# First batch of a threshold attention: transposes by the identity instead of by scaled identities, and another rhythm of the weight conversion

## The chip, the cores and the metric

The kernel runs on one core of a Trainium2 chip. The metric is device microseconds of one execution, the median over several runs. The profile is one such execution, taken by the hardware profiler. In profiles PE is TensorE (its weight loads are PEld), DVE is VectorE, ACT is ScalarE, POOL is GpSimd and SP is SyncE.

## The reference

Two blocks follow each other, all in fp32 results (the three weight matrices arrive as 64-bit floats).

```
# attention: batch 8, heads 8, sequence 576, head size 64
scores = (q @ k^T) / sqrt(64)
thresh = max(scores, last axis) - tau
scores = where(scores >= thresh, scores, -1e9)
attn   = softmax(scores)              # sum + 1e-9 in the denominator
a      = attn @ v                     # (8, 8, 576, 64)
x      = heads side by side           # (4608, 512)
# SwiGLU: 512 -> 1536 -> 512
g   = x @ w_gate
out = (g * sigmoid(g) * (x @ w_val)) @ w_out
```

## The kernel before

**Work units.** The attention goes by head pairs: a pair is two heads of one batch entry, so there are 4 pairs a batch entry and 32 in all. The kernel strings them together as segments. The first batch entry is cut differently from the rest. Segments 0 to 3 hold tiles 0 and 1 (128 rows of q each) of pairs 0 to 3; segments 4 to 7 hold tiles 2, 3 and the short tile 4 (64 rows, both heads in one set of 128 partitions) of the same pairs. From segment 8 on a segment is a whole pair with five tiles, in the "halved" layout. Below, a tile is named by segment and place: 4x1 is the second tile of segment 4.

**One tile of the first batch** (`scores`, not halved). TensorE makes the scores (L301, L306) into two score banks of PSUM, one for each head. VectorE takes the row maximum, negated (`nm`, L326). ScalarE makes the threshold (`th`, L331) and the exponential (L332). VectorE masks it and sums the rows (L336), then makes the reciprocal of the sum (`ri`, L346). The score bank is free for the next tile when L336 has run. So far p is not normalised: ScalarE multiplies the identity matrix by `ri`, one per head (`diags`, L361), and the scaling is done by the transposes.

**The transposes** (`flip`). p has the rows of q on partitions and must have the columns on partitions for the product with v. `flip` does it on TensorE by ordinary products, p as the stationary operand and the scaled identity as the moving one: four blocks of 128x128 into one bank (L389), the last 64 columns into the `end` bank (L391, L395). ScalarE copies them to SBUF (L392, L396, L397). `attend_tile` multiplies them by v one tile later (L412, L416), and ScalarE copies the result into x (L418). From the second batch on none of this is used: there p is scaled by ScalarE (L354) and GpSimd (L352), and VectorE transposes it in 32x32 blocks (L371).

**The weights.** Each weight matrix comes as 64-bit words and must be turned into fp32. It is cut into 24 pieces: 16 of w_gate and w_val (each with 384 columns of both, for 128 rows), 8 of w_out. `fetch_weights` starts the transfers, `split_weights` makes two fp32 parts on ScalarE (L191, L192), `join_weights` puts them together with three operations on VectorE (L200, L202, L203) and one on GpSimd (L205). At most one piece is split in most tiles, and one joined: "one step per tile".

**The fill.** The SwiGLU products are cut into pieces by the generator `block`: `gate` (L481, `pg`), `value` (L481, `pv`), then the output products (L562 for the first two units, L595 for the others). `fill(part)` is called twice per tile and puts as many pieces into TensorE's queue as `pace` allows: the work that is at hand over the tiles that are left. A piece of gate with row block f needs the first 4, 8, 12 or 16 weight pieces; `need` makes them on the spot when they are not there. The first unit of rows is given to the fill in segment 4.

**Order.** All engines work their queues in program order, and the order is written by hand in the loop at the end of the kernel. For each tile: its scores up to the exponential; `attend_tile` for the tile two before; `flip` for the tile before; a weight split; masking and reciprocal; a weight join; fill; scaled identities; fill; and, at the last but one tile of a segment, `prepare` of the next segment (transposes of k and q on VectorE, L767 to L773) and the transfer of the q and k after that, with q multiplied by a constant on GpSimd (L244).

Of the kernel before, what the change touches and what calls it, by code (L numbers as in the profile page):

```python
# [13 lines left out]
AF = mybir.ActivationFunctionType  # L14
ALU = mybir.AluOpType
# [4 lines left out]
def kernel(  # L20
# [30 lines left out]
    nc = tc.nc  # L51
    P = 128
    B, H, S, D = q.shape
    NP = H // 2
# [154 lines left out]
    def need(n):  # L209
        while len(joined) < n:  # L210
            fetch_weights(2)
            if not split:
                split_weights()
            join_weights()
            split_weights()
# [61 lines left out]
    def scores(seg, t):  # L277
        qT, kT, tiles, halved = seg["qT"], seg["kT"], seg["tiles"], seg["halved"]
        if halved and "p" not in seg:
            seg["p"] = arenas[seg["i"] % 2]  # L280
        q0 = t * P - seg["q0"]
        heads = [slice(h * D, (h + 1) * D) for h in range(2)]
        if t < NT:
            pss = [ps_s.tile([P, 2, 512], F32, name="sc") for _ in range(2)]
            at = [t, NT + 1 + t]
        else:
            pss = [ps_s.tile([P, 2, 512], F32, name="sc")]
            at = [t]
        if halved:
            put = [(pss[u], h, q0 + u * D) for u in range(len(pss)) for h in range(2)]  # L290
            for x in range(0, len(put), 2):
                for g in range(NG):
                    a, c = divmod(g, 2)
                    for ps, h, col in put[x:x + 2]:
                        hs = heads[h]
                        nc.tensor.matmul(ps[g * G:(g + 1) * G, h, 0:SH], qT[hs, col + a * G:col + (a + 1) * G],  # L296
                                         kT[hs, c * SH:(c + 1) * SH], start=True, stop=True)
        elif t < NT:
            for h, hs in enumerate(heads):
                for n in range(2):  # L300
                    nc.tensor.matmul(pss[h][:, n, 0:SH], qT[hs, q0:q0 + P], kT[hs, n * SH:(n + 1) * SH],  # L301
                                     start=True, stop=True)
        else:
            for n, h in ((0, 0), (1, 1), (1, 0), (0, 1)):
                hs = heads[h]
                nc.tensor.matmul(pss[0][hs, n, 0:SH], qT[hs, q0:q0 + D], kT[hs, n * SH:(n + 1) * SH],  # L306
                                 start=True, stop=True)
        mx, nm, th, ri = (stp.tile([P, 4, 2] if x == "mx" else [P, 4], F32, name=x) for x in ("mx", "nm", "th", "ri"))
        sm = sums[0]
        sums.rotate(1)  # L310
        if halved:
            m = 2 * len(at)
            scs = [ps[:, h, 0:SH] for ps in pss for h in range(2)]
            ps = [seg["p"][:, x, u * SH:(u + 1) * SH] for u in range(2) for x in at]
            for x, tile_ in enumerate(pss):
                nc.vector.tensor_reduce(out=mx[:, 2 * x:2 * x + 2, 0], in_=tile_[:, :, 0:SH], axis=AX.X, op=ALU.max,  # L316
                                        negate=True)
            meet(mx, m, largest)
            nc.vector.tensor_reduce(out=nm[:, 0:m], in_=mx[:, 0:m, :], axis=AX.X, op=ALU.min)  # L319
        else:  # L320
            m = len(at)
            scs = [ps[:, :, 0:SH] for ps in pss]
            ps = [pbufs[0][:, x, :].rearrange("p (n s) -> p n s", n=2) for x in range(m)]
            pbufs.rotate(1)
            for x in range(m):
                nc.vector.tensor_reduce(out=nm[:, x:x + 1], in_=scs[x], axis=AX.XY, op=ALU.max, negate=True)  # L326
        if halved:
            nc.scalar.activation(th[:, 0:m], nm[:, 0:m], AF.Identity, bias=cut, scale=-1.0)  # L328
        for x in range(m):
            if not halved:  # L330
                nc.scalar.activation(th[:, x:x + 1], nm[:, x:x + 1], AF.Identity, bias=cut, scale=-1.0)  # L331
            nc.scalar.activation(ps[x], scs[x], AF.Exp, bias=nm[:, x:x + 1])  # L332
        yield
        turn(1)
        for x in range(m):
            nc.vector.scalar_tensor_tensor(out=ps[x], in0=scs[x], scalar=th[:, x:x + 1], in1=ps[x],  # L336
                                           op0=ALU.is_ge, op1=ALU.mult, accum_out=sm[:, x, 0:1])
        tot = stp.tile([P, 4], F32, name="tot")
        if halved:
            yield  # L340
            meet(sm, m, same)
            yield
            nc.vector.tensor_reduce(out=tot[:, 0:m], in_=sm[:, 0:m, :], axis=AX.X, op=ALU.add)
        else:
            nc.vector.tensor_reduce(out=tot[:, 0:m], in_=sm[:, 0:m, 0:3:2], axis=AX.X, op=ALU.add)
        nc.vector.reciprocal(out=ri[:, 0:m], in_=tot[:, 0:m])  # L346
        if not halved:
            yield
        if halved:
            for x in range(m):  # L350
                if x % 2:
                    nc.gpsimd.tensor_scalar(out=ps[x], in0=ps[x], scalar1=ri[:, x:x + 1], scalar2=None, op0=ALU.mult)  # L352
                else:
                    nc.scalar.activation(ps[x], ps[x], AF.Copy, scale=ri[:, x:x + 1])  # L354
            unturned.append([seg["p"][:, x, :] for x in at])
        else:

            diags = dbufs[0][:, 0:m, :]
            dbufs.rotate(1)
            for x in range(m):  # L360
                nc.scalar.activation(diags[:, x, :], ident, AF.Copy, scale=ri[:, x:x + 1])  # L361
            unflipped.append((seg, t, [(p.rearrange("p n s -> p (n s)"), diags[:, x, :]) for x, p in enumerate(ps)]))
            yield
        yield

# [10 lines left out]
    def flip():  # L376

        if not unflipped:
            return
        seg, t, ps = unflipped.popleft()  # L380
        n = P if t < NT else D
        pT = pTbufs[0][:, 0:2 * KT * n].rearrange("p (h t q) -> p h t q", h=2, t=KT)
        pT2 = pTbufs[0][:, 2 * KT * n:(2 * KT + 1) * n]
        pTbufs.rotate(1)
        end = ps_f.tile([P, 512], F32, name="end", tag="psf")
        for h, (p, diag) in enumerate(ps):
            tp = ps_f.tile([P, 512], F32, name="tp", tag="psf")
            for kt in range(KT):
                nc.tensor.matmul(tp[:, kt * P:(kt + 1) * P], p[:, kt * P:(kt + 1) * P], diag, start=True, stop=True)  # L389
            if t < NT:  # L390
                nc.tensor.matmul(end[h * D:(h + 1) * D, 0:P], p[:, KM:S], diag, start=True, stop=True)  # L391
                nc.scalar.copy(pT[:, h], tp.rearrange("p (t q) -> p t q", q=P))  # L392
            else:
                for hs in (slice(0, D), slice(D, P)):
                    nc.tensor.matmul(end[hs, 0:D], p[hs, KM:S], diag[hs, hs], start=True, stop=True)  # L395
                nc.scalar.copy(pT, tp.rearrange("p (t h q) -> p h t q", h=2, q=D))  # L396
        nc.scalar.copy(pT2, end[:, 0:n])  # L397
        unattended.append((seg, t, pT, pT2))
# [88 lines left out]
    def gate(j, cs, f, hts, gts):  # L487
# [4 lines left out]
        if f % per == 0:  # L492
            gt = gp.tile([P, 2, TC], F32, name="gt").rearrange("p f n -> p (f n)")
            gts[f // per] = gt[:, 0:per * n].rearrange("p (f n) -> p f n", n=n)
        need(NCC * ((f + GR - 1) * P // FW + 1))
        ps = yield from rows_of_products(j, cs, f, 0, "pg")
        nc.scalar.copy(gts[f // per][:, f % per:f % per + GR, :], ps)  # L497
        yield HCOST
# [194 lines left out]
    def start_batch(b):  # L693
# [8 lines left out]
        if b % BT == 0:  # L702
            while ("last", b // BT - 1) in xts:
# [8 lines left out]

    flat = pall.rearrange("p n s -> p (n s)")
    pbufs = deque(pall[:, 8 + 2 * x:10 + 2 * x] for x in range(2))
    dbufs = deque(flat[:, NP * (S - QA) + 2 * P * x:NP * (S - QA) + 2 * P * (x + 1)].rearrange("p (h q) -> p h q", h=2)
                  for x in range(2))
    pTbufs = deque(flat[:, (12 + 2 * x) * S:(14 + 2 * x) * S] for x in range(2))
    segs = [{"i": i, "tiles": early, "halved": False} for i in range(NP)]
    segs += [{"i": i, "tiles": rest, "halved": False} for i in [NP - 1, *range(NP - 1)]]
    segs += [{"i": i, "tiles": ([2, 3, 0, 1] if i % 2 else [0, 1, 2, 3]) + [NT], "halved": True} for i in range(NP, NPAIR)]  # L720
    assert (2 * KT + 1) * P <= 2 * S and NP == NT == 4 and NP * (S - QA + P) <= 4 * S
    gains = []
    for n, seg in enumerate(segs):
        seg["gives"] = supply(n // NP - 1) if n % NP == NP - 1 and n >= NP else []
# [69 lines left out]
    for n, seg in enumerate(segs):  # L794
        if NP <= n < 2 * NP:
            seg["v"] = segs[seg["i"]]["v"]
        for x, t in enumerate(seg["tiles"]):
# [11 lines left out]
            if attends and n > 2 * NP:  # L809
# [2 lines left out]
                    start_batch(prev["i"] // NP)  # L812
                products = attend(prev)
            part = pace(n, x) / 2
            more = len(split)
            if n or x:
                split_weights()
                fetch_weights(2)
            if x == 0 and n >= NP:
                fetch_qk(seg["i"] + 1)  # L820
            next(go)
# [5 lines left out]
                sigmoids()  # L827
            fill(part)
            next(go)
            if attends and n > 2 * NP:  # L830
                next(products)
                next(products)
                give(n - 1)
# [49 lines left out]
```

## Time and profile before

| | |
|---|---|
| time | 1569.68 us, median of 3 runs (1569.26 to 1570.92) |
| span in the profile | 1568.6 us, granted TensorE clock 0.991 |
| instructions | 31607 |
| first scores of tile 0x1 | 13.03 us from the start |
| first scores of tile 4x1 | 69.45 us |
| first scores of the second batch (segment 8) | 157.97 us |

The page gives, for the whole span, the busy time of each engine and its busy share in 40 slices of 39 us each. The tables of windows give busy us by engine for any stretch. In a timeline, a line has start, duration, engine, line of the kernel, operation, what it writes and reads, and in brackets how long its engine was idle before it and what released it.

### The profile page before, as it was taken

The numbers are of one execution on the slowest core, as the hardware profiler recorded it, in microseconds if no ns is written. First come the engines' busy times: TensorE is split into PE (matmuls) and PEld (weight loads), VectorE is DVE, ScalarE is ACT, GpSimd is POOL, SyncE is SP. The second block draws the span as 40 slices with busy tenths as digits, with TensorE's granted clock in tenths as the row PEclk, the third lists the DMA queues.
The fourth block names the chain that finished last, engine by engine and source line by source line (L and its number), as shares of the span: only waits on it lengthen the run. The fifth ranks groups of instructions, "written<-read, shape, count | busy, mean of one in ns | idle before, by whom it ended". The sixth has DMA issues, their size and how long they took to land. (4 is left out here: it accounts for less than half of the span.)

```text
span 1568.6 us, 31607 instructions
## 1 busy us (share of the span) xinstructions
PE 1509.2 (96%) x11872; PEld 1141.3 (73%) x11872; DVE 1022.2 (65%) x3150; ACT 832.2 (53%) x2165; POOL 628.3 (40%) x638
## 2 busy tenths in 40 slices
PE   7999878999999999999999999999999999899998
PEld 5777554467677767777777777777777777788887
DVE  6866877777677757774767777777676777412212
ACT  5767766546465555654555555474647464511110
POOL 2313543336546354633454544363536263500011
PEclk9999999999999999999999999999999999999999
DMA  8533311211111111110211111111011120000000
GB/s 189 142 99 102 95 28 31 56 43 30 24 45 45 31 32 45 43 34 1 45 32 45 31 45 31 45 32 36 12 42 31 45 46 15 1 14 0 14 14 14
DMA packets 176489, 66.93 MB, mean 43 GB/s; under 512 B 159696, under 2 KB 159696, under 8 KB 176336
## 3 DMA queue, kind: packets, MB, share of 16 engines
q1 hardware_dynamic: 168656, 54.88, 15.7%
q0 software_dynamic: 2944, 9.44, 1.7%
q8 instruction: 94, 1.54, 0.4%
q10 hardware_dynamic: 4736, 0.59, 0.3%
q14 instruction: 59, 0.48, 0.1%
HBM read 55.44 MB, written 9.44 MB: 41 GB/s over the span
## 5 line engine op out<-in xcount | busy, mean ns | idle before, releaser
L481 PE MATMUL pv<-xall,wgv 128*128 128x256 f32 x1728 | 405.7, 386 | 0.0
L481 PE MATMUL pg<-xall,wgv 128*128 128x256 f32 x1728 | 399.9, 382 | 0.0
L481 PEld LDWEIGHTS pv<-xall,wgv 128*128 128x128 f32 x1728 | 328.4, 192 | 67.0 <-issue 21.7
L481 PEld LDWEIGHTS pg<-xall,wgv 128*128 128x128 f32 x1728 | 323.5, 190 | 66.4 <-issue 19.0
L352 POOL TENSOR_SCALAR pall<-pall,ri 128x288 f32<-128x288 f32 x252 | 249.9, 1002 | 258.3 <-DVE ri L346 234.0
L336 DVE SCALAR_TENSOR_TENSOR pall<-sc,th,pall 128x288 f32<-128x288 f32 (+1 forms) x540 | 258.6, 529 | 63.6 <-ACT pall L332 63.6
L332 ACT ACTIVATE pall<-sc,nm 128x288 f32<-128x288 f32 (+1 forms) x540 | 236.1, 509 | 0.5
L296 PE MATMUL sc<-kT,qT 64*32 64x288 f32 x4032 | 161.6, 416 | 34.8 <-DVE pall L336 33.3
L316 DVE TENSOR_REDUCE mx<-sc 128x2 f32<-128x576 f32 x252 | 177.7, 742 | 22.3 <-PE sc L296 21.1
L371 DVE STREAM_TRANSPOSE pall<-pall 128x576 f32<-128x576 f32 x252 | 181.9, 754 | 10.7 <-POOL pall L352 10.7
L522 POOL TENSOR_TENSOR ht<-ht,gt 128x512 f32<-128x512 f32 x84 | 104.7, 1272 | 200.9 <-ACT gt L520 200.9
L275 ACT COPY sums<-sums 32x4 f32<-32x4 f32 (+1 forms) x560 | 108.5, 194 | 143.7 <-DVE pall L336 134.2
L595 PE MATMUL po<-wo,ht 128*128 128x256 f32 x768 | 176.8, 382 | 0.0
L595 PEld LDWEIGHTS po<-wo,ht 128*128 128x128 f32 x768 | 144.9, 191 | 28.0 <-issue 4.6
L354 ACT ACTIVATE pall<-pall,ri 128x288 f32<-128x288 f32 x252 | 122.2, 527 | 69.6 <-DVE ri L346 68.5
L504 DVE TENSOR_TENSOR ht<-gt,pv 128x512 f32<-128x512 f32 x102 | 69.8, 685 | 125.0 <-PE pv L481 116.2
L328 ACT ACTIVATE th<-nm,cut 128x4 f32<-128x4 f32 (+1 forms) x140 | 41.2, 295 | 206.1 <-DVE nm L319 206.0
L296 PEld LDWEIGHTS sc<-kT,qT 64*32 64x32 f32 x4032 | 58.6, 106 | 114.7 <-issue 83.5
L438 PE MATMUL xa<-pall,vall 64*64 64x288 f32 x2016 | 130.2, 405 | 0.7 <-issue 0.6
L438 PEld LDWEIGHTS xa<-pall,vall 64*64 64x64 f32 x2016 | 77.8, 133 | 49.1 <-issue 5.8
L608 POOL TENSOR_TENSOR ht<-ht,xall 128x256 f32<-128x256 f32 x48 | 34.7, 726 | 184.5 <-PE po L595 182.2
L497 ACT COPY gt<-pg 128x512 f32<-128x512 f32 x108 | 63.5, 588 | 79.7 <-PE pg L481 77.3
(102 smaller groups left out, 1477.0 us busy)
## 6 DMA issues: line engine op xcount, KB each, us to landing
vall<-in_v_dram SPq DMA_DIRECT2D x112, 144.0 KB, 3.4
qraw<-in_q_dram SPq DMA_DIRECT2D x116, 72.0 KB, 2.5
kraw<-in_k_dram SPq DMA_DIRECT2D x116, 72.0 KB, 2.9
out_dram<-ob POOLq DMA_DIRECT2D x32, 256.0 KB, 2.4
wo<-in_moe_w_gate_dram SPq DMA_DIRECT2D x16, 384.0 KB, 3.8
wo<-in_moe_w_val_dram SPq DMA_DIRECT2D x16, 384.0 KB, 4.3
xall<-in_moe_w_out_dram SPq DMA_DIRECT2D x5, 768.0 KB, 4.6
wo<-in_moe_w_out_dram SPq DMA_DIRECT2D x3, 768.0 KB, 4.8
```

The source lines that it names most:

```text
L275: nc.scalar.copy(out, in_[:, :, 0])
L296: nc.tensor.matmul(ps[g * G:(g + 1) * G, h, 0:SH], qT[hs, col + a * G:col + (a + 1) * G], kT[hs, c * SH:(c + 1) * SH], start=True, stop=True)
L316: nc.vector.tensor_reduce(out=mx[:, 2 * x:2 * x + 2, 0], in_=tile_[:, :, 0:SH], axis=AX.X, op=ALU.max, negate=True)
L332: nc.scalar.activation(ps[x], scs[x], AF.Exp, bias=nm[:, x:x + 1])
L336: nc.vector.scalar_tensor_tensor(out=ps[x], in0=scs[x], scalar=th[:, x:x + 1], in1=ps[x], op0=ALU.is_ge, op1=ALU.mult, accum_out=sm[:, x, ...
L352: nc.gpsimd.tensor_scalar(out=ps[x], in0=ps[x], scalar1=ri[:, x:x + 1], scalar2=None, op0=ALU.mult)
L354: nc.scalar.activation(ps[x], ps[x], AF.Copy, scale=ri[:, x:x + 1])
L371: nc.vector.transpose(out=p, in_=p)
L438: nc.tensor.matmul(xa[a][h * D:(h + 1) * D, at:at + n * G].rearrange("d (i q) -> d i q", q=G), vr[rs, h, j, :], p[rs, lo:lo + n, j, :], st ...
L481: nc.tensor.matmul(ps[:, i], wgv[:, mat, c, (f + i) * P:(f + i + 1) * P], x[:, c, cs], start=(c == 0), stop=(c == NCC - 1))
L522: eng.tensor_tensor(out=ht, in0=ht, in1=gt[:, 2 * y:2 * y + 2, :], op=ALU.mult)
L595: nc.tensor.matmul(ps, h(f), w[:, f, :], start=(f == 0), stop=(f == NF2 - 1))
```

## The change

Three edits, all for the first batch. The transposes use the identity in TensorE's transpose mode, so p is scaled beforehand: the first head of a tile by ScalarE, the second by GpSimd, as in the later batches; the scaled identities and their buffers go. The weight steps get another rhythm: in segments 0 to 3 one per two tiles, with the split and the join in the same (second) tile; from segment 4 on one per tile, and in segments 4 to 7 a second one in the short tile. And a gate piece whose weights are not joined yet makes the fill pass instead of forcing them.

```diff
         nc.vector.reciprocal(out=ri[:, 0:m], in_=tot[:, 0:m])
-        if not halved:
-            yield
+        for x in range(m):
+            if x % 2:
+                nc.gpsimd.tensor_scalar(out=ps[x], in0=ps[x], scalar1=ri[:, x:x + 1], scalar2=None, op0=ALU.mult)
+            else:
+                nc.scalar.activation(ps[x], ps[x], AF.Copy, scale=ri[:, x:x + 1])
         if halved:
...
         else:
-
-            diags = dbufs[0][:, 0:m, :]
-            dbufs.rotate(1)
-            for x in range(m):
-                nc.scalar.activation(diags[:, x, :], ident, AF.Copy, scale=ri[:, x:x + 1])
-            unflipped.append((seg, t, [(p.rearrange("p n s -> p (n s)"), diags[:, x, :]) for x, p in enumerate(ps)]))
+            unflipped.append((seg, t, [p.rearrange("p n s -> p (n s)") for p in ps]))
+            yield
             yield
         yield
...
-        for h, (p, diag) in enumerate(ps):
+        for h, p in enumerate(ps):
             tp = ps_f.tile([P, 512], F32, name="tp", tag="psf")
             for kt in range(KT):
-                nc.tensor.matmul(tp[:, kt * P:(kt + 1) * P], p[:, kt * P:(kt + 1) * P], diag, start=True, stop=True)
+                nc.tensor.transpose(tp[:, kt * P:(kt + 1) * P], p[:, kt * P:(kt + 1) * P], ident)
             if t < NT:
-                nc.tensor.matmul(end[h * D:(h + 1) * D, 0:P], p[:, KM:S], diag, start=True, stop=True)
+                nc.tensor.matmul(end[h * D:(h + 1) * D, 0:P], p[:, KM:S], ident, start=True, stop=True)
...
-        need(NCC * ((f + GR - 1) * P // FW + 1))
+        while len(joined) < NCC * ((f + GR - 1) * P // FW + 1):
+            yield 0
...
             more = len(split)
-            if n or x:
+            if n >= NP or x:
                 split_weights()
                 fetch_weights(2)
+            if n < NP:
+                more = x
...
             fill(part)
             next(go)
+            if t == NT and NP <= n < 2 * NP:
+                join_weights()
+                split_weights()
+                fetch_weights(2)
```

More of the change, by code (lines that the diff above doesn't have):

```diff
@@ L346, in scores @@
         nc.vector.reciprocal(out=ri[:, 0:m], in_=tot[:, 0:m])
-        if not halved:
-            yield
-        if halved:
-            for x in range(m):
[L351 to L354, printed above, removed]
+        for x in range(m):
[3 more added lines that the diff above has]
+                nc.scalar.activation(ps[x], ps[x], AF.Copy, scale=ri[:, x:x + 1])
+        if halved:
             unturned.append([seg["p"][:, x, :] for x in at])
         else:
-            diags = dbufs[0][:, 0:m, :]
-            dbufs.rotate(1)
-            for x in range(m):
-                nc.scalar.activation(diags[:, x, :], ident, AF.Copy, scale=ri[:, x:x + 1])
-            unflipped.append((seg, t, [(p.rearrange("p n s -> p (n s)"), diags[:, x, :]) for x, p in enumerate(ps)]))
+            unflipped.append((seg, t, [p.rearrange("p n s -> p (n s)") for p in ps]))
+            yield
             yield
@@ L394, in flip @@
                 for hs in (slice(0, D), slice(D, P)):
-                    nc.tensor.matmul(end[hs, 0:D], p[hs, KM:S], diag[hs, hs], start=True, stop=True)
+                    nc.tensor.matmul(end[hs, 0:D], p[hs, KM:S], ident[hs, hs], start=True, stop=True)
                 nc.scalar.copy(pT, tp.rearrange("p (t h q) -> p h t q", h=2, q=D))
@@ L714 @@
     pbufs = deque(pall[:, 8 + 2 * x:10 + 2 * x] for x in range(2))
-    dbufs = deque(flat[:, NP * (S - QA) + 2 * P * x:NP * (S - QA) + 2 * P * (x + 1)].rearrange("p (h q) -> p h q", h=2)
-                  for x in range(2))
     pTbufs = deque(flat[:, (12 + 2 * x) * S:(14 + 2 * x) * S] for x in range(2))
@@ L720 @@
     segs += [{"i": i, "tiles": ([2, 3, 0, 1] if i % 2 else [0, 1, 2, 3]) + [NT], "halved": True} for i in range(NP, NPAIR)]
-    assert (2 * KT + 1) * P <= 2 * S and NP == NT == 4 and NP * (S - QA + P) <= 4 * S
+    assert (2 * KT + 1) * P <= 2 * S and NP == NT == 4
     gains = []
```

## The prediction

> **What bounds the kernel now.** I read the page first (engine shares, slices), then a table of three stretches, then TensorE's waits in each, then the timeline of one tile. From the page:
>
> ```profile
> PE 1509.2 (96%) x11872; PEld 1141.3 (73%) x11872; DVE 1022.2 (65%) x3150; ACT 832.2 (53%) x2165; POOL 628.3 (40%) x638
> PE   7999878999999999999999999999999999899998
> ```
>
> TensorE is busy nearly throughout, so work taken from it counts wherever it never waits. The first slices (39 us each) and the dip at slices 5 and 6 are the places where it may wait. The change touches only the first batch: segments 0 to 3 (two tiles each), segments 4 to 7 (three tiles each), and a little of what follows. I cut there: first scores of tile 0x1 (segment 0, tile 1) to those of 4x1, from there to the first scores of the second batch, and onward. Busy us of each engine:
>
> ```profile
> core 0: us, PE busy (x) PEld busy (x) DVE busy (x) ACT busy (x) POOL busy (x), PEclk, DMA share, GB/s
> 13.03:69.45 56.42, 55.25 (x400) 41.44 (x400) 46.42 (x99) 43.71 (x98) 18.64 (x11) 1.00 0.73 186
> 69.45:157.97 88.52, 87.53 (x638) 66.41 (x637) 57.63 (x116) 61.06 (x128) 23.68 (x14) 1.00 0.31 98
> 157.97:330.00 172.03, 146.83 (x1277) 86.64 (x1280) 135.00 (x435) 109.07 (x291) 72.72 (x64) 0.95 0.23 53
> ```
>
> TensorE's waits, first in the middle stretch, then in the late one:
>
> ```profile
> PE tp L389 <- ACT xall L418: 0.8, 2, 0.4
> PE tp L389 <- ACT gt L497: 0.2, 1, 0.2
> ```
>
> ```profile
> PE sc L296 <- DVE pall L336: 23.5, 12, 3.4
> ```
>
> So there are three regimes. The middle stretch (88.5 us) is bound by TensorE: it waits 1.0 us in all, while VectorE and ScalarE have 31 and 27 us to spare. The late stretch has TensorE waiting 23.5 us for VectorE to free the score banks. The early stretch looks TensorE-bound by busy time, but the timeline of tiles 2x1 and 3x0 says otherwise:
>
> ```profile
> 47.78 1.72 POOL L244 TENSOR_SCALAR qraw<-qraw,scl 128x576 f32<-128x576 f32 x1 [4.10 <-DMA qraw<-in_q_dram]
> 47.88 1.46 DVE L203 SCALAR_TENSOR_TENSOR wgv<-wo,wgv 128x768 uint32<-128x768 uint32 x1
> ...
> 52.86 0.17 DVE L346 RECIPROCAL ri<-tot 128x2 f32<-128x2 f32 x1
> 52.92 0.96 ACT L191 ACTIVATE wgv<-wo 128x768 f32<-128x768 f32 x1
> 52.94 0.54 DVE L200 TENSOR_SCALAR wgv<-wgv 128x768 f32<-128x768 f32 x1
> 53.51 0.56 DVE L202 TENSOR_SCALAR wgv<-wgv 128x768 uint32<-128x768 uint32 x1
> ...
> 54.11 0.96 DVE L203 SCALAR_TENSOR_TENSOR wgv<-wo,wgv 128x768 uint32<-128x768 uint32 x1
> ...
> 54.99 1.41 DVE L326 TENSOR_REDUCE nm<-sc 128x1 f32<-128x576 f32 x2
> ```
>
> VectorE goes from one tile's reciprocal straight into a weight join (L200 to L203, 52.94 to 54.99, 2.05 us) and from that straight into the next tile's maximum: only 0.33 us of a tile's 5.73 (reciprocal at 53.03 to reciprocal at 58.76) is idle. The early stretch is VectorE's. The last thing to see is L203 at 47.88: 1.46 us beside a GpSimd operation where it takes 0.96 alone.
>
> What the transposes cost on TensorE, from the middle stretch:
>
> ```profile
> 81.14 1.16 PE L389 MATMUL tp<-pall 128*128 128x128 f32 x8
> 82.23 0.43 PE L391 MATMUL end<-pall 128*64 128x128 f32 x2
> 82.59 3.72 PE L481 MATMUL pg<-xall,wgv 128*128 128x256 f32 x16
> ```
>
> Four products leave eight records: each fp32 product is two passes of weights and data, 0.145 us a record, 0.29 us a block. One head's p costs 82.59 - 81.14 = 1.45 us with its end piece.
>
> **What the Trainium skill says.** "TensorE: Matmul & The Clock Gate", section Terms, says that on trn2 a weight load and a matmul have a transpose mode, four times faster for FP32; "Perfetto Trace Analysis", section Transposes, asks that a logical transpose use it and not a standard matmul. No run here has shown it yet; what agrees is that a plain fp32 product costs two records. "TensorE: Matmul & The Clock Gate", Part 4, warns that transposes may not count as activity for the clock; no trace here shows that. "SBUF — State Buffer", section Who interferes with whom, says that GpSimd and VectorE share a port pair; the 1.46 against 0.96 us of L203 agrees that they disturb each other.
>
> **The change, part by part.**
> (1) Transposes by the identity. 36 p, four blocks each; the end pieces stay plain products. A block now costs 0.29. Four times less is 0.07; one record at today's pace instead of two is 0.145. I take the middle, 0.11 (bounds 0.07 and 0.29, the last if the mode brings nothing here). The middle stretch holds 152 records, 76 blocks: 76 x 0.18 = 13.7 us less. In the early stretch the saving (64 blocks) is hidden behind VectorE.
> (2) Scaling of p. Two scaled identities (L361, 0.42 each, 0.35 at back-to-back pace) leave ScalarE; one 128x576 scaling enters it per tile, which I price as the exponential of that shape (L332, 0.72): +1.7 us over the 11 tiles of the middle stretch. GpSimd gets one 128x576 scaling per two-head tile, priced by L244 at 1.72: 7 x 1.72 = 12 us onto 23.7 of 88. New wait: the second head's transposes now wait for GpSimd. Its scaling stands before the tile's join in the queue; it can stand behind a q scaling (L244) that waits for its DMA, as at 47.78. Behind the waiting transposes stand that tile's fill products and the next scores. The scaling ends about 1.9 us after the reciprocal, while now the second head's blocks start 3.7 us after it (reciprocal of tile 3x1 ends at 58.76, its second head's blocks start at 62.49), so I cost it at nothing. But it runs beside the join of the same tile on VectorE: up to 0.5 us per hit operation, about 0.7 us per tile, 5 us on VectorE in the middle stretch.
> (3) Weight steps. By the order of the instructions, up to the scores of 4x1: joins 7 to 4, splits (L191 + L192, 1.96) 8 to 5. Middle stretch: joins 11 to 15, splits 11 to 15. Late: joins 6 to 5.
> Early: VectorE gives up 3 x 2.06 = 6.2 us, but in the remaining join tiles the split is issued in the same tile, so L200 waits for ScalarE: the reciprocal ends at 53.03, L191 only at 53.88, about 1.0 us per join with the new order, 3 us. Net 3.2; less 0.7 for GpSimd beside the joins: 2.5 us gained.
> Late: one join less, 2.06 us, where VectorE is what TensorE waits for: 2 us gained.
> (4) The gate no longer forces joins but lets the fill pass. By the order of TensorE one group of four gate/value products (8 records at 3.72/16 = 0.23 us, 1.9 us) less comes before the second batch, and it is made up within that batch's first tiles, in the late stretch, where TensorE waits anyway: 1.9 us less in the middle, nothing lost.
>
> Middle stretch then: TensorE 88.5 - 13.7 - 1.9 = 72.9; ScalarE 61.1 + 4 x 1.96 + 1.7 = 70.6; VectorE 57.6 + 4 x 2.06 + 5 = 70.8. Three engines within 4% of each other: tiles are uneven (a short tile has two weight steps, others more fill), so the bound alternates, and the stretch can't be as short as the largest sum. I add 6.1 us (about half a microsecond for each of 11 tiles) and get 79.0: 9.5 us gained.
> Sum: 2.5 + 9.5 + 2 = 14 us; 1569.7 - 14 = 1555.7, rounded to 1556.
>
> **The rivals.**
> A. The transpose mode brings nothing for fp32 (0.29 a block). For: no trace shows it. Against: the skill names it. Early 2.5, middle 1.9, late 2: 6.4 us, 1563.
> B. The mode works, but ScalarE and VectorE, now at 71 us with more weight steps just there, take over, and waits between them stretch the middle to 85: gain 2.5 + 3.5 + 2 = 8, time 1562. For: the closeness of the sums. Against: both have slack now of 27 to 31 us.
> C. Slower: the mode brings nothing or costs the clock, and each of 11 tiles waits some 1 us for the GpSimd scaling that stands behind a q scaling or is slowed by VectorE: middle 86.6 + 11 = 97.6, 9 us lost, against 4.5 gained: 1574. For: L244 idled 4.1 us for its DMA in the middle of the queue. Against: in segments 4 to 7 no q is fetched until the last, and the slack before the second head is 2 us.
>
> **How the numbers follow.** Forecast 0.6, A 0.12, B 0.14, C 0.11, and 0.03 for no change that can be measured. Low end: block at 0.07 (3 us more), the full 3 us of the early stretch, and less unevenness: 1546. High end: past A and B, 1568. Faster by over 0.2% (3.1 us): the forecast, B and most of A, 0.83; same: the rest of A and of the forecast's neighbourhood, 0.05; slower 0.12.
>
> **What would show it.** In the changed profile: one record per block on the tp line instead of two, at 0.07 to 0.15 us; the stretch between the scores of 4x1 and of the second batch at about 80 us, with TensorE, ScalarE and VectorE all near 90% there; first scores of 4x1 about 2.5 us earlier; waits of sc on L336 in the late stretch below 23.5 by about 2. I am wrong if tp blocks keep 0.29, if tp waits for the GpSimd scaling by more than a few us in sum, or if the middle stretch stays above 85.

## The result, and the profile after

The changed kernel takes **1583.97 us** (median of 5 runs, 1583.55 to 1585.77) where the kernel before took 1569.26 beside it (5 runs, 1568.32 to 1570.92): a ratio of 1.0096, 95% interval 1.0081 to 1.0111. It is 15 us slower. The forecast was 1556.

From the page of the changed kernel, the engine shares and two of the lines in 40 slices:

```profile
PE 1501.3 (95%) x11728; PEld 1124.4 (71%) x11728; DVE 1032.8 (65%) x3150; ACT 836.3 (53%) x2149; POOL 658.2 (42%) x654
...
PE   6888788989999999999999999999999999899998
...
PEclk9889899999999999999999999999999999999999
```

TensorE has 144 records fewer and 8 us less busy time, and each of the first five slices is emptier than before. The granted clock, which the windows of the kernel before showed at 1.00 from 13 to 158 us, has its dips (8s) among the first five slices. Three stretches, cut at the same events as before (first scores of tile 0x1, of tile 4x1, of the second batch) and, for the third, at the first scores of the third pair of the second batch (segment 10), busy us of each engine:

```profile
core 0: us, PE busy (x) PEld busy (x) DVE busy (x) ACT busy (x) POOL busy (x), PEclk, DMA share, GB/s
13.06:72.90 59.84, 51.08 (x336) 34.20 (x336) 41.70 (x90) 39.96 (x83) 29.19 (x17) 0.91 0.57 141
72.90:165.44 92.54, 81.09 (x553) 57.13 (x552) 69.79 (x124) 66.74 (x125) 41.14 (x23) 0.93 0.35 112
165.44:251.95 86.51, 69.25 (x602) 48.30 (x601) 69.93 (x205) 58.29 (x142) 41.01 (x32) 0.90 0.26 60
```

The kernel before from its first scores of the second batch to those of segment 10:

```profile
157.97:237.88 79.91, 65.02 (x598) 47.55 (x597) 66.21 (x200) 55.41 (x138) 38.90 (x31) 0.96 0.24 58
```

The early stretch took 56.42 us and takes 59.84; the middle took 88.52 and takes 92.54, although 85 TensorE records left it; the first two pairs of the second batch took 79.91 and take 86.51. All three are longer, and what follows them is about as long as before. The middle was TensorE's with 1.0 us of waits; now TensorE is idle for 11.5 us of it. What it waits for, over the first 400 us (total, times, longest):

```profile
PE sc L296 <- DVE pall L336: 27.5, 11, 6.5
PE sc L301 <- DVE qT L761: 8.0, 1, 8.0
PE pg L475 <- POOL wgv L205: 6.5, 2, 5.5
PE sc L301 <- DVE pall L336: 5.8, 3, 2.7
PE tp L383 <- ACT xall L412: 4.6, 2, 3.6
PE tp L383 <- POOL pall L349: 2.9, 1, 2.9
PE xa L406 <- ACT pall L386: 2.0, 1, 2.0
```

The 8.0 is the start of the kernel, before the first cut. Of the others, the gate products waiting for a weight piece (`pg` for L205) and the transposes waiting for a scaling (`tp` for L349) were not among the waits of before at all; the wait for the copy into x (L412, formerly L418) was 0.8 us and is 4.6; the wait of the second batch (L296) grew from 23.5 to 27.5.

The largest new wait is in the timeline between tiles 5x0 and 5x1:

```profile
91.63 0.70 PE L475 MATMUL pg<-xall,wgv 128*128 128x256 f32 x2 [0.93 <-POOL wgv L205]
...
92.69 0.93 ACT L191 ACTIVATE wgv<-wo 128x768 f32<-128x768 f32 x1
...
93.30 0.54 DVE L200 TENSOR_SCALAR wgv<-wgv 128x768 f32<-128x768 f32 x1
93.47 1.01 ACT L192 ACTIVATE extra<-wo,minus 128x768 f32<-128x768 uint32 x1
93.55 1.87 POOL L349 TENSOR_SCALAR pall<-pall,ri 128x576 f32<-128x576 f32 x1 [1.98 <-DVE ri L346]
93.87 0.98 DVE L202 TENSOR_SCALAR wgv<-wgv 128x768 uint32<-128x768 uint32 x1
...
94.89 0.96 DVE L203 SCALAR_TENSOR_TENSOR wgv<-wo,wgv 128x768 uint32<-128x768 uint32 x1
...
96.00 1.80 POOL L205 TENSOR_TENSOR wgv<-wgv,extra 128x768 uint32<-128x768 uint32 x1 [0.57 <-DVE wgv L203]
...
97.85 1.22 PE L475 MATMUL pg<-xall,wgv 128*128 128x256 f32 x2 [5.52 <-POOL wgv L205]
99.00 1.47 PEld L301 LDWEIGHTS sc<-pall 64*128 64x128 f32 x8 [0.65 <-issue]
99.00 2.30 PE L301 MATMUL sc<-pall 64*128 64x288 f32 x8
```

Read it upward from 97.85: the last two gate records wait for the sum L205 (96.00), that for L203, L202, L200 of the join. The program counts a piece as joined as soon as it has written the join's instructions; the products that need it then stand in TensorE's queue ahead of the next tile's scores, and those go late with them. L202 takes 0.98 us beside L349 on GpSimd (0.56 alone in the kernel before). The eight score records at 99.00 then take 2.30 us; the same eight took 1.25 at 72.90. So the stall goes on after its end. The windows just after it:

```profile
97.85:105.00 7.15, 7.15 (x41) 4.49 (x42) 3.22 (x7) 2.94 (x8) 0.00 (x0) 0.56 0.23 87
105.00:112.00 7.00, 7.00 (x51) 4.98 (x50) 4.15 (x7) 4.23 (x8) 3.76 (x2) 1.00 0.37 112
```

TensorE is busy in all of the first 7.15 us, at a granted clock of 0.56, and the clock is back at 1.00 after. This wait costs itself and a slow stretch behind it.

### The profile page after: what moved, and what is told of

The parts are those of the page before. It is cut to its first block, busy times and chain, and to the rows that moved or that the text cites. A ratio compares the mean times of both kernels' runs of the same rounds, so it can differ in the third digit from the quotient of the medians.

```text
span 1582.2 us, 31311 instructions
## 1 busy us (share of the span) xinstructions
PE 1501.3 (95%) x11728; PEld 1124.4 (71%) x11728; DVE 1032.8 (65%) x3150; ACT 836.3 (53%) x2149; POOL 658.2 (42%) x654
## 5 line engine op out<-in xcount | busy, mean ns | idle before, releaser
L475 PE MATMUL pg<-xall,wgv 128*128 128x256 f32 x1728 | 406.3, 386 | 6.5 <-POOL wgv L205 6.5
L349 POOL TENSOR_SCALAR pall<-pall,ri 128x288 f32<-128x288 f32 (+1 forms) x268 | 279.0, 1051 | 296.3 <-DVE ri L346 272.7
L336 DVE SCALAR_TENSOR_TENSOR pall<-sc,th,pall 128x288 f32<-128x288 f32 (+1 forms) x540 | 258.6, 529 | 63.3 <-ACT pall L332 63.3
L296 PE MATMUL sc<-kT,qT 64*32 64x288 f32 x4032 | 161.6, 416 | 39.6 <-DVE pall L336 37.7
L351 ACT ACTIVATE pall<-pall,ri 128x288 f32<-128x288 f32 (+1 forms) x272 | 138.0, 546 | 70.6 <-DVE ri L346 69.5
L296 PEld LDWEIGHTS sc<-kT,qT 64*32 64x32 f32 x4032 | 58.8, 106 | 119.2 <-issue 86.4
```

The source lines that it names most:

```text
L475: nc.tensor.matmul(ps[:, i], wgv[:, mat, c, (f + i) * P:(f + i + 1) * P], x[:, c, cs], start=(c == 0), stop=(c == NCC - 1))
```

## The experiments

Line numbers in the L300s and L400s are those of the changed kernel (those after the gate stand one line earlier in the variants with forced joins). Stretches and waits are those of one profiled run each. Each ratio is against the kernel before, run again beside each group of experiments (medians 1569.26 to 1569.72 us). Two theories stood against each other. **Weights:** the slow start of the weight steps makes TensorE wait in segments 0 to 5. **Scaling:** the transposes, short as they are, wait for p scaled on GpSimd. First the two halves of the change, each by itself.

**e1: the transposes and the scaling alone,** weight steps and forced joins as before.

```diff
-        while len(joined) < NCC * ((f + GR - 1) * P // FW + 1):
-            yield 0
+        need(NCC * ((f + GR - 1) * P // FW + 1))
...
-            if n >= NP or x:
+            if n or x:
...
-            if n < NP:
-                more = x
...
-            if t == NT and NP <= n < 2 * NP:
-                join_weights()
-                split_weights()
-                fetch_weights(2)
```

> The changed transposes and scaling with the weight steps and the forced gate of before. Theory W (the new weight rhythm costs the time: TensorE waits 6.5 us for joined weights, its clock drops after the waits, and second steps collide): clearly faster than before, 1558 to 1565, no wait of pg on L205, granted clock back at 0.99. Theory G (scaling p on GpSimd costs it, by waits of tp on L349 and by slowing VectorE): still slower than before, 1574 or more, with the waits of tp on L349 kept.

**e2: the weight steps and the passing gate alone,** transposes by scaled identities (the same four edits, made to the kernel before in the other direction).

> The new weight rhythm and the passing gate with the transposes of before (scaled identities, nothing on GpSimd for p). Theory W: slower than the changed kernel or as slow, 1580 to 1592, with waits of pg on L205 kept. Theory G: about as before, 1566 to 1573.

**e3: the changed kernel with forced joins** (only the first of the four edits of e1).

> The changed kernel, but a gate piece whose weights are missing forces them again. If passing (fill lost in tiles whose weights are late) is the costly part: 1570 to 1576. If the weights being late at all is it, forcing only moves the wait: 1580 to 1590, since a forced piece is split, joined and waited for on the spot.

Measured: e1 1572.93 us, ratio 1.0021 (1.0014 to 1.0028); e2 1586.65, 1.0104 (1.0087 to 1.0121); e3 1582.71, 1.0086 (1.0069 to 1.0102). Both halves lose, the weights about 17 us, the transposes 3. Their sum is larger than the 15 of both together; what they share is not shown. Passing or forcing makes no difference in the time that these runs tell (the intervals of e3 and of the change overlap). It does move the loss: with forced joins the middle stretch is 98.4 us and the first two pairs of the second batch 79.3, against 92.5 and 86.5. In e2, where the transposes are the old ones, the wait for weights is there all the same, 5.0 us in one piece:

```profile
PE pg L481 <- POOL wgv L205: 5.0, 1, 5.0
```

**e5: the changed kernel with one weight step per tile in segments 0 to 3** again; the second steps in short tiles and the passing gate stay.

```diff
-            if n >= NP or x:
+            if n or x:
...
-            if n < NP:
-                more = x
```

> The changed kernel, but with one weight step per tile in segments 0 to 3 as before; the second step of short tiles and the passing gate stay. If the slow start of the weights is what costs in the new rhythm: 1568 to 1575, near the run with the transposes alone (1572.9), no wait of pg on L205. If the second steps of the short tiles (joins beside the GpSimd addition of the one before) cost it: still 1579 or more.

Measured: 1571.08 us, ratio 1.0011 (1.0004 to 1.0018), 12.9 us less than the changed kernel, and the waits of `pg` for L205 are gone. So the slow rate in segments 0 to 3 costs some 13 us, and the other two weight edits are not what costs: e1 lacks them, and e5 is 1.9 us below it, barely more than the scatter. The stretches of e5, from the first scores of 4x1 and from those of the second batch:

```profile
73.35:162.57 89.22, 80.73 (x561) 57.81 (x560) 70.27 (x126) 68.38 (x127) 42.55 (x24) 0.98 0.33 107
162.57:240.49 77.92, 64.59 (x593) 45.22 (x593) 61.55 (x195) 51.53 (x135) 34.12 (x29) 0.96 0.23 47
```

The early stretch of e5 is as long as the changed kernel's (59.9 us). The middle is 3.3 us shorter, and the first two pairs of the second batch are 8.6 us shorter.

**e13: which of two ways it costs.** The slow rate stays, but in segments 1 to 3 the split stands one tile ahead of its join, so that there no join waits for a split of its own tile. (Segment 0 keeps both in its second tile.)

```diff
-            if n >= NP or x:
+            if n >= NP or x == (n == 0):
```

> The changed kernel, with its one weight step per two tiles in segments 0 to 3, except that the split stands one tile ahead of its join (in segments 1 to 3 the split in the first tile, the join in the second), so that no join waits for the split of its own tile. As many pieces are joined at the end of segment 3 as in the changed kernel. Theory W (what the slow start costs is mostly the join that waits for its split in the same tile: L200 waits for L191 by 6.4 us in sum): 1576 to 1580, first scores of 4x1 about 3 us earlier. Theory L (what it costs is that the pieces are late for the gate products of segments 4 and 5): 1582 to 1585, with the waits of pg for L205 as in the changed kernel (5 to 7 us).

Measured: 1579.54 us, ratio 1.0064 (1.0052 to 1.0077), 4.4 us less. Both theories had a part: the first scores of 4x1 come at 69.79 instead of 72.90, and the joins wait for the split by 0.9 us (once, in segment 0) instead of 6.4 (in the changed kernel: `DVE wgv L200 <- ACT wgv L191`, four times). But the waits for weights are unchanged:

```profile
PE pg L475 <- POOL wgv L205: 6.5, 2, 5.5
```

Of the 13 us, 4.4 are thus the join behind its split. The rest, some 8.5, is what is left of the slow rate, and no run divides it. The traces name two parts. One is the late pieces: 6.5 us of TensorE waits for weights, and the slow clock behind them. The other is the backlog: joins that are not made in segments 0 to 3 have to be made later. By the count of L200, 5 joins are left when VectorE turns to the second batch in the changed kernel and in e13, and 2 in e5. VectorE is busy for 69.93 us of the first two pairs in both, 61.55 in e5, and there TensorE waits for VectorE by 16.7 us (12.7 in e5). But the kernel before has 6 joins left and takes 79.91 us, so the count alone doesn't explain it. In e13 the middle (92.52) is only 3.3 us longer than in e5, the first two pairs (88.20) 10.3. So most of the loss shows up after the waits for weights, but part of it may be work that they pushed back.

**e6: as e1, with both heads scaled by ScalarE** in the first batch. **e8: as e1, with GpSimd scaling only from segment 4 on.**

```diff
-            if x % 2:
+            if halved and x % 2:
```

```diff
-            if x % 2:
+            if x % 2 and (halved or t >= TA):
```

> As the transposes alone, but both heads of the first batch scaled by ScalarE, none by GpSimd. Theory W: within 3 us of the run with the transposes alone, either way (0.72 us more on ScalarE for each two-head tile against a free port for VectorE). Theory G: at least 5 us faster than it.

> The transposes alone, but GpSimd scales the second heads only from segment 4 on; in segments 0 to 3 ScalarE scales both. The 6.0 us between 1572.9 (GpSimd) and 1566.9 (ScalarE): if they come from GpSimd's queue standing at the q scaling that waits for its DMA, which is in segments 0 to 3 alone: 1565 to 1569. If they come from GpSimd and VectorE slowing each other, in all segments: half of it stays, 1569 to 1572.

Measured: e6 1566.94 us, ratio 0.9984 (0.9977 to 0.9991), faster than the kernel before; e8 1570.08, 0.9997 (0.9987 to 1.0007). Against e1 the GpSimd scaling costs 6.0 us, roughly half of it in segments 0 to 3 (e8 scatters over 7 us, so the share is rough; in the profiles the early stretch is 59.2 us in e1 and 56.5 in e6). How it costs there is seen in the changed kernel's timeline, for the p of tile 0x1:

```profile
19.52 0.17 DVE L346 RECIPROCAL ri<-tot 128x2 f32<-128x2 f32 x1
...
23.28 0.66 PE L383 MATMUL tp<-ident,pall 128*128 128x128 f32 x4
...
23.73 1.72 POOL L244 TENSOR_SCALAR extra<-extra,scl 128x576 f32<-128x576 f32 x1 [7.78 <-DMA extra<-in_q_dram]
...
25.43 1.72 POOL L349 TENSOR_SCALAR pall<-pall,ri 128x576 f32<-128x576 f32 x1
...
27.20 0.66 PE L383 MATMUL tp<-ident,pall 128*128 128x128 f32 x4 [2.90 <-POOL pall L349]
```

The reciprocal is there at 19.69. The scaling L349 stands in GpSimd's queue behind the q scaling L244, which waits 7.78 us for a transfer, so it starts at 25.43; the second head's transposes wait 2.90 us, and the next tile's scores stand behind them. In e1 the same wait is 4.1 us. For the other half, in segments 4 to 7, these traces have no wait of `tp` for L349; that VectorE runs slower beside GpSimd is the candidate, and no run isolates it.

**What is left of e6's waits.** In e6 the middle stretch takes 85.26 us, and TensorE still waits 2.6 us (`tp` for the copy L412) and 1.9 (`tp` for `gt`, the copy of `pg`, L491). `tp` shares four PSUM banks with the fill products, and ScalarE, which empties them, is held up by the sigmoids (in the changed kernel two loads of function tables, 1.28 us each, and the wait of 3.65 at 137.18). Theory: with short transposes the banks come round sooner, and ScalarE's copies become the wait. **e9: e6 with the copy L412 on VectorE. e10: the kernel before with the same edit,** where TensorE has hardly a wait to lose.

```diff
-        nc.scalar.copy(xts[("last", 0) if t == NT ...
+        nc.vector.tensor_copy(xts[("last", 0) if t == NT ...
```

> The transposes alone, scaled by ScalarE, and the copy of the product with v (L412) on VectorE in place of ScalarE. Theory R (the time saved on TensorE is lost since the PSUM banks of the fill come free late, behind ScalarE's exponentials, and each such wait also drops the clock): 1558 to 1564, waits of tp on the copies gone. Rival (TensorE is held by other things, the supply of fill or the late stretch): 1565 to 1569.

> The kernel before with the same copy (there L418) on VectorE. Theory R: nothing, 1567.5 to 1571, since TensorE, with the longer transposes, came to the banks when they were free (1.0 us of such waits in all). Rival: it gains as much here as with the short transposes.

Measured: e9 1564.12 us, ratio 0.9965 (0.9952 to 0.9978); e10 1569.04, 0.9995 (0.9986 to 1.0003). The edit brings 2.8 us with the new transposes and nothing that can be told without them. The waits of `tp` for L412 fall to 0.6 us; the 1.9 us for `gt` stay, now of `pv`.

**e11: e9 with ordinary products in place of the transpose mode,** to price the mode by itself. p is still scaled beforehand.

```diff
-                nc.tensor.transpose(tp[:, kt * P:(kt + 1) * P], p[:, kt * P:(kt + 1) * P], ident)
+                nc.tensor.matmul(tp[:, kt * P:(kt + 1) * P], p[:, kt * P:(kt + 1) * P], ident, start=True, stop=True)
```

> As the version with all scaling on ScalarE and the product of v copied by VectorE (1564.1), but the four blocks of each head are transposed by ordinary products with the identity again, not in the transpose mode. Theory M (the mode itself is what pays, one pass of 0.147 us a block instead of two): the blocks go back to 1.16 us per four, 76 blocks x 0.145 = 11 us of the middle stretch are TensorE's again and the time rises towards the kernel before plus the cost of scaling p, 1569 to 1572. Theory N (the mode costs the clock as much as it saves, the 5 us came from the other edits): the time stays at 1564 to 1566 with the granted clock above 0.99 in the middle.

Measured: 1570.54 us, ratio 1.0003 (0.9995 to 1.0011). The mode is worth 6.4 us here. One tile's transposes, first with ordinary products (e11), then in the mode (e9); start, duration, records:

```profile
80.76 1.16 PE L383 MATMUL tp<-ident,pall 128*128 128x128 f32 x8
81.85 0.43 PE L385 MATMUL end<-ident,pall 128*64 128x128 f32 x2
82.21 1.16 PE L383 MATMUL tp<-ident,pall 128*128 128x128 f32 x8
```

```profile
78.59 0.66 PE L383 MATMUL tp<-ident,pall 128*128 128x128 f32 x4
79.18 0.43 PE L385 MATMUL end<-ident,pall 128*64 128x128 f32 x2
79.54 0.66 PE L383 MATMUL tp<-ident,pall 128*128 128x128 f32 x4
```

One record a block instead of two, and 0.95 us from one head to the next instead of 1.45: 0.50 for four blocks, 0.125 a block. The middle stretch of e11 and then of e9, columns as in the windows above:

```profile
70.52:157.84 87.32, 87.32 (x638) 66.41 (x637) 60.64 (x127) 66.38 (x119) 25.52 (x15) 1.00 0.33 104
```

```profile
69.36:149.81 80.45, 77.93 (x561) 55.97 (x561) 60.25 (x127) 65.94 (x119) 25.37 (x15) 1.00 0.34 109
```

TensorE loses 77 records and 9.4 us of busy time, and the stretch 6.9 us. VectorE and ScalarE do the same work in both. The clock is 1.00 in both, so the mode doesn't lower it by itself; Part 4 of the Trainium skill's page "TensorE: Matmul & The Clock Gate", which warns that transposes may not count as activity, isn't borne out at this density of transposes (76 blocks in 80 us).

**e12: e9 with the second steps in short tiles and the passing gate added,** that is, the two weight edits that e5 had cleared.

> The best version so far (transposes in the mode, all scaling of p on ScalarE in the first batch, VectorE copies the product of v, 1564.1) with two parts of the change added: the second weight step in the short tiles of segments 4 to 7, and the gate piece that lets the fill pass. Segments 0 to 3 keep one weight step per tile. Theory S (the second steps take weight work out of the second batch, where TensorE waits for VectorE): 1561 to 1563, with the waits of sc for L336 below the 27.2 us of the version without them. Theory T (second steps fill VectorE and ScalarE just where the shortened transposes need them): 1565 to 1568.

Measured: 1563.06 us, ratio 0.9962 (0.9948 to 0.9976). The median is the lowest of all, though e9 and e12 can't be told apart in time. The waits of `sc` for L336 in the second batch (L296) fall as the theory of the second steps has it, from 27.2 us in e9 (first) to 23.1 (second). The middle stretch grows from 80.45 to 84.69 us, and the first two pairs of the second batch fall from 82.90 to 76.38: the second steps move time from the one into the other.

```profile
PE sc L296 <- DVE pall L336: 27.2, 13, 3.4
```

```profile
PE sc L296 <- DVE pall L336: 23.1, 12, 3.6
```

## Why the prediction was wrong

By stretches, in us of the profiled runs:

| stretch | forecast | measured |
|---|---|---|
| early, to the first scores of 4x1 | 2.5 gained | 3.4 lost |
| middle, to those of the second batch | 9.5 gained | 4.0 lost |
| the rest | 2 gained | 6.1 lost |

**Step 3, the weight rhythm: the step that failed.** It counted three joins less on VectorE in segments 0 to 3 as 2.5 us gained, and one less in the second batch as 2. The slow early rate cost 13 (e5). The 1.0 us per join that it set down for L200 behind L191 was 1.6 on average (6.4 in four) and cost 4.4 us of time (e13). The larger part, 8.5, was not in the working at all. A weight piece has a deadline, the gate products of segments 4 and 5, and TensorE waited 6.5 us at it; and joins put off crowd a later place. The step compared loads (fewer joins here, more there) and never asked when each piece is needed. How the 8.5 divides between the two stays open. The early gain itself does show where the joins no longer stand behind their splits: e13 reaches the first scores of 4x1 3.6 us before e5, in one profile each. Its reading that VectorE bounds the early stretch holds in the main, though TensorE was as full there (55.25 of 56.42 us): with the mode TensorE has 4.6 us less to do in this stretch, and it shortens by 1.1 only (57.24 us in e11, 56.16 in e9).

**Step 2, the scaling on GpSimd, "cost at nothing": wrong by 6.0 us** (e1 against e6). The step had named the very wait, behind a q scaling that waits for its transfer, and set it aside because the second head's blocks start 3.7 us after the reciprocal. For tile 0x1 the scaling only started 5.7 us after it (19.69 to 25.43). Disturbance of VectorE was put at up to 0.5 us an operation. Beside L349 it was 0.42 (0.98 against 0.56 at 93.87); beside the sum L205 L202 reached 2.06 us, 1.5 more (at 86.57), where a second join stands in the same tile. ScalarE does the scaling of both heads without any of this: with all of it, it is busy for 65.94 of 80.45 us in the middle of e9. Rival C came nearest in sign and named this wait, but for another place: it put 1 us into each of the 11 tiles of the middle, where the traces have none, and its mode that brings nothing was wrong. It too counted 4.5 us gained from the weights, where they lost.

**Step 1, the transposes: the mechanism right, the size too large.** One record a block, as forecast. But the term was 0.18 us saved per block, and it is 0.125: 76 blocks make 9.5 us instead of 13.7. A block takes about 0.165 us where 0.11 was set down; the fourfold speed that the prediction cites, 0.07, did not show, 0.29 to 0.165 is 1.8 times. Rival A (the mode brings nothing) is out: 6.4 us.

**Step 4, the passing gate, "nothing lost":** stands for the whole time as far as the runs tell (e3).

**The late stretch, 2 us gained:** not so, 6.1 lost, all in the first two pairs. The waits for L336 rose from 23.5 to 27.5 us, the longest from 3.4 to 6.5, and the granted clock in the first two pairs fell from 0.96 to 0.90. By the timeline VectorE comes late to the second batch: two joins stand ahead of its first maxima (before, one), the later one stretched by GpSimd beside it (L200 at 166.15 takes 1.66 us, L203 at 168.44 2.06), and the first maximum starts 5.0 us after the first scores instead of 0.8. So part of this loss is work of the middle that ends behind the cut. Without the slow start the same second steps and the passing gate do lower these waits by 4.1 us (e12 against e9).

**The middle sum.** 79.0 us was forecast, 92.54 measured. The transposes without the slow weights and the GpSimd scaling have 85.26 (e6, in a profiled run 2.2 us above its median), with ScalarE's copies as the wait, much as rival B had it; 80.45 is reached only with the copy moved besides (e9), so its nearness to 79.0 is luck. What the sum for the changed kernel lacked was TensorE's waits: 11.5 us there, 6.5 for weights and 4.6 for the copy into x, and the lower clock (0.93 over the stretch). An unevenness spread at half a microsecond per tile was no substitute for looking for the one place that stalls for 5.5.

## What to carry to other kernels

When a background job (here the weight conversion) is thinned out, list when each of its results is needed and compare that with when it will be ready; comparing engine loads before and after says nothing of it. And ask what stands where the work that was put off will land. When work moves to another engine, read what stands ahead of it in that engine's queue, a wait for a transfer above all, and prefer the engine whose queue has none. A saving on the bounding engine is worth only what the next waits leave of it: 9.4 us of TensorE time became 6.4 here, and of that 2.8 came with moving a copy that empties a PSUM bank off the busy ScalarE.

## What the hardware showed that was not expected

After a wait of 5.5 us on TensorE the granted clock was 0.56 over the next 7.15 us (eight score records 2.30 us instead of 1.25). A shorter wait can do it too: after the wait of 3.65 us that ended at 137.18 in the changed kernel, eight gate records took 3.65 us, where at 128.08 they took 1.99. Not every wait does: after the 2.90 us that ended at 27.20 the clock was 1.00 up to 32.00, and eight score records took 1.25. VectorE's shift L202 takes 0.56 us alone, 0.98 beside a scaling with one tensor on GpSimd and up to 2.06 beside an addition of two tensors there (L205).
